# A new order of one head pair's work on all engines of an attention and mixture-of-experts kernel

## The chip, the core and the metric

The kernel runs on one core of a Trainium2 chip. It uses five engines with instruction streams of their own: TensorE (PE in the profile; its weight loads are listed apart, as PEld), VectorE (DVE), ScalarE (ACT), GpSimd (POOL) and SyncE (SP), which issues most of the DMAs. Each engine works through its instructions in the order in which the program wrote them, and waits where one needs a result of another engine. The metric is the time of one execution on the device in microseconds.

## The reference

Attention over 8 batches of 8 heads, 576 positions and 64 columns a head, with a learned bias (a small network of one hidden layer of 32, fed with log distances) that depends on the positions alone, and behind it a mixture of 8 experts, of which each token takes the best one, weighted with its probability `gate_w`.

```python
def _attn_ref(q, k, v, w1, b1, w2):
    scores = scale * np.matmul(q, k.transpose(0, 1, 3, 2))
    ...
    scores = scores + bias.transpose(2, 0, 1)[None, :, :, :]
    scores = scores - np.max(scores, axis=-1, keepdims=True)
    attn = np.exp(scores)
    attn = attn / (np.sum(attn, axis=-1, keepdims=True) + 1e-09)
    return np.matmul(attn, v).astype(np.float32)

def _moe_ref(x, modality_id, w_gate, modality_bias, w1, w2):
    logits = x @ w_gate + modality_bias[modality_id]
    e_idx = np.argmax(logits, axis=1)
    ...
    for e in range(E):
        h = np.maximum(x[mask] @ w1[e], 0.0)
        out[mask] = gate_w[mask, None] * (h @ w2[e])
```

## The kernel before

The kernel has three stages: a table of the bias is built (to about 65 us), attention runs over 32 pairs of heads (to about 602 us), and the experts' products follow. The change lies in the attention stage.

A pair of heads is two heads of one batch, side by side on the 128 partitions. Its 576 rows are cut into five chunks: chunks 0 to 3 of 128 rows, for each head on its own, and chunk 4, the last 64 rows of both heads together. One pair takes these steps, each with a letter in the order table. A capital starts a step on TensorE, and the small letter of the same step is the copy of its result out of PSUM.

- P0, P1, P2: q, k and the last rows of both are transposed (`prep`). H (ScalarE) writes the high part of the result, and G (VectorE) the low part; scores are made of three products of these parts.
- S0 to S4: the scores of a chunk (`scores`, L411), followed on VectorE by one pass a head that adds the bias and finds the row's extreme (`biased`, L434). The scores of both heads stand in `sps0` and `sps1`; S4 uses `sps0` alone. The passes write to one of four slots of `Eb`.
- E: the exponential of one chunk and head on ScalarE, in place (`exps`, L448). C: a copy of the last 64 columns on GpSimd (`compact`, L453).
- T0 to T4: the transposes of a chunk (`etrans`, L322, for chunk 4 L462). R and N: those of the last 64 columns (`rtrans`, L322, and `rtrans4`, L499). Their copies are t, r and n (L327 on ScalarE, L329 on VectorE).
- A0 to A3: four column pieces of the product with v (`av`, L523), 128, 144, 160 and 144 columns wide (`CUT`). Copied by a.
- L and V: loads of q and k, and of v, issued by SP. X, Y, O, Z and D: steps of the routing of a finished batch, which run beside the following pairs: Y logits and ranks, X their transposes and the token rows', O small operations on VectorE, Z scatters issued by GpSimd, D stores of the token rows.

The order in which the program writes all this is a table, `ORDER`: five strings, walked through once for each pair n by `attention`. A + behind a step means the pair n+1, a - the pair n-1, two signs two pairs. What follows the colon is the PSUM place of a step, or for a small letter the engine of the copy (a ScalarE, v VectorE; without it the default, both engines with one bank each for t and r, and ScalarE for a and n). TensorE's results besides the scores have four PSUM banks: `eps0` and `eps1` (e, or e0, e1), and `xps0` and `xps1` (x). T0 to T3 fill both banks of a letter, and an A takes one bank. Whoever fills a bank waits until the copy of what stood there is done. Other work hangs on the ends of the five strings by the string's number: the late blocks of the bias table at the first pair, and the first tables, row loads and weights of the experts' stage at the last four.

Of the kernel before, what the change touches and what calls it, by code (L numbers as in the profile page):

```python
# [23 lines left out]
D = 64  # L24
H = 8
NP = H // 2
HID = 32
S4 = S // 4
# [81 lines left out]
class Attn:  # L110
# [155 lines left out]
    def attn_early(self, st, rst):  # L266
# [22 lines left out]
        for k in range(2):  # L289
# [3 lines left out]
            qk = cp.tile([P, 2, P], F32, name=f"qkrem{k}")  # L293
            nc.vector.memset(qk, 0.0)
            self.qkrem.append(qk)
        self.qraw, self.kraw, self.vmain, self.E, self.rem, self.sums, self.xT = {}, {}, {}, {}, {}, {}, {}

    def attn_late(self, st):

# [212 lines left out]
    def av(self, n, part, u):  # L512

        nc = self.nc
        if part == 0:
            self.xT[n] = self.xTb[n // NP % 2][:, n % NP, :]
        v, eT, rT = self.vmain[n], self.eTs[n % 2], self.rT
        sl = slice(self.CUT[part], self.CUT[part + 1])
        ps = self.banks[u[0]][int(u[1])][:, 0 : sl.stop - sl.start]
        for k in range(5):  # L520
            for h in range(2):
                o = slice(64 * h, 64 * h + 64)
                nc.tensor.matmul(  # L523
                    ps[o, :],
                    v[:, h, k, :] if k < 4 else self.vrem[n % 2][:, o],
                    eT[:, h, k, sl] if k < 4 else rT[:, sl],
                    start=k == 0,
                    stop=k == 4,
                    tile_position=(0, 64 * h),
                    skip_group_check=True,  # L530
                )
        if part == 3:
            del self.vmain[n]
        dst = self.xT[n][:, sl]
        return lambda by=0: self.copy(by, dst, ps)

    def first_steps(self, route):
# [34 lines left out]


    ORDER = (
# [5 lines left out]
    )  # L580

    def attention(self):
# [47 lines left out]
        for n in range(n_pair + 2):  # L630
            for u in range(5):
# [5 lines left out]
                for op in self.ORDER[u].split():  # L637
# [9 lines left out]
                    elif op in ("x", "y"):  # L647
                        self.route_evac(op.upper())
                    elif 0 <= m < n_pair and not (n > n_pair and op[0] in "CV"):
                        pair[op[0]](m, *(int(x) for x in op[1:].strip("+-")), *([to] if to else []))  # L650
        while self.scatters:
            self.route_scatter()

# [989 lines left out]
```

## Time and profile before

| | |
|---|---|
| median of 3 runs | 1063.31 us (1060.08 to 1065.63) |
| the profiled execution | 1065.25 us, of which the span from the first to the last instruction is 1063.5 us |
| granted TensorE clock, mean | 0.988 of full speed |
| TensorE, matmuls | 1003.6 us busy, 94% of the span |
| TensorE, weight loads | 843.5 us, 79% |
| VectorE | 749.6 us, 70% |
| ScalarE | 683.5 us, 64% |
| GpSimd | 216.1 us, 20% |

Busy time is the union of the spans of an engine's instructions. Matmuls are pipelined, so that the next one starts before the last has ended, and the end of a matmul is modelled: the distance between two starts tells more than a length. In the rows, `xps<-idf,kraw 64*128 64x64` is a matmul into `xps` whose weights are 64 rows by 128 columns of the array; in brackets stands how long the engine had been idle, and what ended that.

### The profile page before, as it was taken

To read this page: it belongs to the slowest core of one execution; us is meant where nothing else is said; L and a number is where in the kernel's file an instruction comes from. 1 tells how busy PE (TensorE), PEld (TensorE's weight loads), DVE (VectorE), ACT (ScalarE), POOL (GpSimd) and SP (SyncE) were. 2 spreads that over 40 slices of the span, in tenths; PEclk is the share of its full clock that TensorE was granted. 3 is DMA by queue.
4 is the path that set the end of the run, shared out by engine and by line. 5 is a ranking of instruction groups with operands and counts; after the bars stand their busy time and mean duration, and the time that the engine had idled before them with its cause. 6 is when DMAs were issued, how large, how long until landed. Compare 5 with 4: busy or idle time off the path is not lost. (4 is left out here: it accounts for less than half of the span.)

```text
span 1063.5 us, 29967 instructions
## 1 busy us (share of the span) xinstructions
PE 1003.6 (94%) x11606; PEld 843.5 (79%) x11606; DVE 749.6 (70%) x1785; ACT 683.5 (64%) x1576; POOL 216.1 (20%) x371
## 2 busy tenths in 40 slices
PE   6978999998999999999998899999999999999996
PEld 3447888887888788887877788888888798988995
DVE  7976778877788787888887466985545455555554
ACT  6776787876878777887877454455535355454453
POOL 0000111212222122231323322421111112111120
PEclk9998999999999999999999999999999999999999
DMA  6973222324424334232337101224455511111111
GB/s 164 216 161 67 65 59 57 93 60 75 91 69 78 61 77 86 69 87 62 93 78 180 47 31 41 66 68 136 137 194 199 180 42 60 40 50 41 43 59 32
DMA packets 125036, 93.49 MB, mean 88 GB/s; under 512 B 94097, under 2 KB 102673, under 8 KB 124884
## 3 DMA queue, kind: packets, MB, share of 16 engines
q1 hardware_dynamic: 117268, 71.19, 26.6%
q0 software_dynamic: 7520, 20.30, 6.2%
q8 instruction: 93, 1.52, 0.8%
q14 instruction: 59, 0.48, 0.2%
q10 hardware_dynamic: 96, 0.00, 0.0%
HBM read 141.40 MB, written 19.38 MB: 151 GB/s over the span
## 5 line engine op out<-in xcount | busy, mean ns | idle before, releaser
L448 ACT ACTIVATE Eb<-Eb,mn 128x576 f32<-128x576 f32 x288 | 224.6, 787 | 17.5 <-DVE mn L434 17.1
L434 DVE CUSTOM_DVE_ANT_0 Eb<-sps,NBm 128x576 f32<-128x576 f32 x256 | 183.6, 754 | 20.8 <-PE sps L411 14.3
L411 PE MATMUL sps<-QK 64*128 64x288 f32 x1536 | 151.6, 316 | 16.0 <-ACT QK L334 7.4
L1259 PE MATMUL p<-QK,w1hi 128*128 128x256 f32 x1152 | 162.8, 284 | 1.3 <-ACT w1hi L1232 1.3
L523 PE MATMUL eps<-eT,vraw 128*64 128x144 f32 (+2 forms) x2048 | 156.6, 296 | 5.2 <-ACT eT L327 4.2
L1259 PEld LDWEIGHTS p<-QK,w1hi 128*128 128x128 f32 x1152 | 149.1, 192 | 7.8 <-issue 5.0
L523 PEld LDWEIGHTS eps<-eT,vraw 128*64 128x64 f32 x2048 | 121.7, 139 | 30.6 <-ACT eT L327 14.2
L411 PEld LDWEIGHTS sps<-QK 64*128 64x128 f32 x1536 | 115.8, 190 | 29.1 <-ACT QK L334 10.9
L1262 DVE SCALAR_TENSOR_TENSOR hl<-p,hh 128x512 fp32r<-128x512 f32 x72 | 49.6, 689 | 119.8 <-ACT hh L1261 118.0
L1261 ACT ACTIVATE hh<-p 128x512 fp32r<-128x512 f32 x72 | 43.0, 597 | 123.7 <-PE p L1259 108.3
L329 DVE COPY eT<-eps 128x512 f32<-128x512 f32 x128 | 88.0, 688 | 44.4 <-PE eps L322 40.5
L453 POOL COPY rem<-Eb 128x128 f32<-128x128 f32 x128 | 37.3, 292 | 337.4 <-ACT Eb L448 291.8
L322 PE MATMUL eps<-idf,Eb 64*128 64x64 f32 x2048 | 93.8, 227 | 7.2 <-ACT xTb L327 2.2
L1226 DVE TENSOR_TENSOR w2lo<-NBm,w2hi 128x1024 fp32r<-128x1024 f32 x72 | 89.3, 1240 | 15.2 <-ACT w2hi L1225 14.9
L1285 POOL DMA_INDIRECT out<-mo,idt x36 | 36.6, 1016 | 281.5 <-ACT mo L1284 258.9
L1259 PE MATMUL p<-QK,w1lo 128*128 128x256 f32 x576 | 92.7, 283 | 1.0 <-DVE w1lo L1233 1.0
L322 PEld LDWEIGHTS eps<-idf,Eb 64*128 64x128 f32 x2048 | 80.6, 141 | 11.9 <-ACT xTb L327 5.1
L1226 DVE TENSOR_TENSOR w1lo<-NBm,w1hi 128x1024 fp32r<-128x1024 f32 x72 | 84.9, 1221 | 3.5 <-ACT w1hi L1225 1.0
L1276 PE MATMUL xps<-w2hi,hh 128*128 128x512 f32 x208 | 83.0, 399 | 0.0
L1276 PE MATMUL xps<-w2hi,hl 128*128 128x512 f32 x208 | 81.4, 392 | 0.8 <-DVE hl L1262 0.8
L1259 PEld LDWEIGHTS p<-QK,w1lo 128*128 128x128 f32 x576 | 79.4, 192 | 1.4 <-DVE w1lo L1233 1.4
L327 ACT COPY eT<-eps 128x512 f32<-128x512 f32 x128 | 77.1, 602 | 3.3 <-PE eps L322 2.4
(254 smaller groups left out, 1756.8 us busy)
## 6 DMA issues: line engine op xcount, KB each, us to landing
NBm<-moe_w SPq DMA_DIRECT2D x20, 2048.0 KB
NBm<-moe_w SPq DMA_DIRECT2D x40, 1024.0 KB
NBm<-moe_w SPq DMA_DIRECT2D x32, 512.0 KB
NBm<-xTb SPq DMA_DIRECT2D x32, 288.0 KB
qraw<-q SPq DMA_DIRECT2D x64, 128.0 KB
kraw<-k SPq DMA_DIRECT2D x64, 128.0 KB
vraw<-v SPq DMA_DIRECT2D x32, 256.0 KB
xg<-xrb SPq DMA_DIRECT2D x28, 258.0 KB
```

The costliest lines, as they stand in the source:

```text
L322: self.nc.tensor.transpose(ps[r][0:n, col : col + 64], x[o, :], self.idf[o, o])
L327: self.nc.scalar.copy(out, ps)
L329: self.nc.vector.tensor_copy(out, ps)
L411: nc.tensor.matmul(self.sps[h or 0][:, half, 0:HS], QD[:, a, :] if h is None else QK[o, 0, a, P * c : P * c + P], QK[o, 1, b, ks], start=i ...
L434: nc.vector.tensor_tensor_reduce(out=e.rearrange("p (t w) -> p t w", t=2), in0=ps, in1=nb.rearrange("p (t w) -> p t w", t=2), scale=1.0, s ...
L448: self.nc.scalar.activation(e, e, AF.Exp, bias=mn, scale=-1.0, accum_out=sm)
L523: nc.tensor.matmul(ps[o, :], v[:, h, k, :] if k < 4 else self.vrem[n % 2][:, o], eT[:, h, k, sl] if k < 4 else rT[:, sl], start=k == 0, st ...
L1226: self.nc.vector.tensor_tensor(l, w, h.bitcast(F32), op=ALU.subtract)
L1259: nc.tensor.matmul(ps[:, a, :], w[:, c, fs], x[:, c, :], start=i == 0, stop=i == len(ops) - 1)
L1261: nc.scalar.activation(hh[:, sl, :], ps, AF.Relu)
L1262: nc.vector.scalar_tensor_tensor(hl[:, sl, :], ps, 0.0, hh[:, sl, :].bitcast(F32), op0=ALU.max, op1=ALU.subtract)
L1276: nc.tensor.matmul(ps, h[:, f, sl], m[:, f, :], start=i == 0, stop=i == len(ops) - 1)
```

## The change

`ORDER` is written anew. The steps of a pair are the same, and so is what each computes. In the new table
- A2 and A3 of pair n-2 follow each other, in e0 and x0; before, T3 and S1 stood between them, and A3 used e0;
- P2, P0 of the next pair stand behind S2 as before, but their parts H and G follow before S3, and P1 stands right behind S3; before, it stood behind S4;
- T2 and T1 of pair n stand behind S4, in e and x; T0 (in x) and T3 of the pair before (in e) stand behind S1, with T4;
- the exponentials of chunks 3 and 4 go to the next pair's first string, between the copies t2 and t1;
- A1's and A3's copies are ScalarE's now, and half of R's is VectorE's;
- the routing's X and Y have one place each in other strings, and the loads of q and k stand in the fourth string.

`av` no longer takes part 0 as the first and part 3 as the last: it sets its destination at each part, and counts the parts. Behind the loop the stores that are still waiting are issued.

```diff
     def av(self, n, part, u):
...
-        if part == 0:
-            self.xT[n] = self.xTb[n // NP % 2][:, n % NP, :]
+        self.xT[n] = self.xTb[n // NP % 2][:, n % NP, :]
+        self.av_done[n] = self.av_done.get(n, 0) + 1
...
-        if part == 3:
+        if self.av_done[n] == 4:
             del self.vmain[n]
...
     ORDER = (
-        "T2-:e t2- L++ S0 A2--:e0 a2--:a Y:e1 y X:x E0 T3-:e",
-        "x t3- S1 A3--:e0 N-:e1 E0 E1 n- E1 a3--:v T4-:x R-:x T0:e C0 C1 Z r-:a O",
-        "t4-:a t0 S2 O A0-:e1 a0-:a E2 P2+:x E2 P0+:x",
-        "H2+ T1:e H0+ V t1 S3 E3 C2 G0+ A1-:e1",
-        "a1-:v E3 S4 P1+:x H1+ G1+ G2+ O Z C3 O E4 D",
+        "E3- t2- E3- S0 O t1- E4- A2--:e0 A3--:x0 a2--:a E0 E0 C3- X:e O x R-:x r- S1 a3-- T4-:e t4-:a",
+        "T0:x E1 T3-:e t0 t3- E1",
+        "S2 P2+:x P0+:x",
+        "N-:e1 H0+ G0+ A0-:e1 E2 O E2 n-:a L++ S3 P1+:x Z a0- A1-:e0 V H1+ D H2+ G1+ C0 Y:e1",
+        "y G2+ S4 a1- C2 O Z T2:e T1:x C1",
     )
...
+        self.route_store()
         while self.scatters:
             self.route_scatter()
```

What stands in a row on TensorE, from A2 of a pair to the transposes behind S1 (here at pair 15; `Eb` holds the scores, `eT` their transposes, `rem` the last columns, `rT` the transposed ones). Before:

```order
L523 MATMUL eps0_739<-eT1_106,vraw13_4762 64x160 x8
L523 MATMUL eps0_739<-rT_107,vrem1_114 64x160 x2
...
L322 MATMUL eps0_739<-idf_62,Eb_88 128x64
...
L411 MATMUL sps0_737<-QK1_73 128x288
...
L523 MATMUL eps0_739<-eT1_106,vraw13_4762 64x144 x8
L523 MATMUL eps0_739<-rT_107,vrem1_114 64x144 x2
L499 MATMUL eps1_740<-idf_62,Eb_88 64x64 x2
L462 MATMUL xps0_77<-idf_62,Eb_88 128x64 x4
...
L322 MATMUL xps0_77<-idf_62,rem14_0_4993 128x64
```

A2 is followed by T3 into the same bank, then S1, A3, N, T4 and R; T0 comes next, and S2. The same stretch after:

```order
L523 MATMUL eps0_739<-eT1_106,vraw13_4776 64x160 x8
L523 MATMUL eps0_739<-rT_107,vrem1_114 64x160 x2
L523 MATMUL xps0_77<-eT1_106,vraw13_4776 64x144 x8
L523 MATMUL xps0_77<-rT_107,vrem1_114 64x144 x2
...
L322 MATMUL xps0_77<-idf_62,rem14_0_5092 128x64
...
L411 MATMUL sps0_737<-QK1_73 128x288
...
L462 MATMUL eps0_739<-idf_62,Eb_88 128x64 x4
...
L322 MATMUL xps0_77<-idf_62,Eb_88 128x64
...
L322 MATMUL eps0_739<-idf_62,Eb_88 128x64
```

A3 has moved up behind A2, into the other bank, R ahead of S1, and T4, T0 and T3 stand between S1 and S2, T4 and T3 in the same bank.

On ScalarE, around the parts of the next pair's q and k (`QK0` from `xps`, L336 with the scale for q, L334 for k; `mn15_6` is pair 15's chunk 3, first head, `mn15_8` chunk 4). Before:

```order
L336 ACTIVATE QK0_72<-xps0_77 128x4x64
L336 ACTIVATE QK0_72<-xps1_78 128x4x64
L327 COPY eT1_106<-eps0_739 128x8x64
L448 ACTIVATE Eb_88,sums15_5187<-Eb_88,mn15_6_5406 128x576
L448 ACTIVATE Eb_88,sums15_5187<-Eb_88,mn15_7_5408 128x576
L334 CAST QK0_72<-xps0_77 128x4x64
L334 CAST QK0_72<-xps1_78 128x4x64
L448 ACTIVATE Eb_88,sums15_5187<-Eb_88,mn15_8_5433 128x576
L327 COPY eT1_106<-eps0_739 128x8x64
L327 COPY xTb1_98<-eps0_739 128x160
```

The parts of k come behind both exponentials of chunk 3, and are followed by that of chunk 4, by T2's copy and by A2's. After:

```order
L336 ACTIVATE QK0_72<-xps1_78 128x4x64
L448 ACTIVATE Eb_88,sums15_5162<-Eb_88,mn15_4_5317 128x576
L448 ACTIVATE Eb_88,sums15_5162<-Eb_88,mn15_5_5319 128x576
L327 COPY rT_107<-eps1_740 128x64
L327 COPY xTb1_98<-eps1_740 128x128
L334 CAST QK0_72<-xps0_77 128x4x64
L334 CAST QK0_72<-xps1_78 128x4x64
L336 ACTIVATE QD0_108<-xps0_77 128x64
...
L327 COPY xTb1_98<-eps0_739 128x144
L448 ACTIVATE Eb_88,sums15_5162<-Eb_88,mn15_6_5378 128x576
```

The parts of k stand behind the exponentials of chunk 2 and the copies of N and A0, ahead of A1's copy, and the exponential of chunk 3 comes behind all of them.

## Rows read from the trace of the kernel before

**Rows 1.** The page: busy time of each engine, share of span, instructions.

```profile
PE 1003.6 (94%) x11606; PEld 843.5 (79%) x11606; DVE 749.6 (70%) x1785; ACT 683.5 (64%) x1576; POOL 216.1 (20%) x371
```

**Rows 2.** Windows: busy time in plain pairs; last TensorE clock, DMA share, GB/s.

```profile
129.00:145.00 16.00, 15.02 (x241) 12.83 (x243) 12.24 (x36) 13.07 (x40) 1.18 (x4) 1.00 0.24 57
```

**Rows 3.** Timeline, TensorE, one pair: start, length, engine, line, tiles, count, idle before.

```profile
111.73 1.06 PE L411 MATMUL sps<-QK,QD 128*128 128x288 f32 x6
112.73 0.46 PE L322 MATMUL xps<-idf,kraw 64*128 64x64 f32 x8
113.03 0.66 PE L322 MATMUL eps<-idf,Eb 64*128 64x64 f32 x16
113.92 1.44 PE L411 MATMUL sps<-QK 64*128 64x288 f32 x12 [0.24 <-ACT QK L334]
115.29 1.31 PE L523 MATMUL eps<-eT,vraw 128*64 128x160 f32 x16
...
117.27 0.71 PE L322 MATMUL eps<-idf,Eb 64*128 64x64 f32 x16 [0.39 <-ACT xTb L327]
117.78 1.04 PE L411 MATMUL sps<-QK 64*128 64x288 f32 x12
118.76 1.20 PE L523 MATMUL eps<-eT,vraw 128*64 128x144 f32 x16
...
120.03 0.28 PE L499 MATMUL eps<-idf,Eb 128*64 128x64 f32 x4
120.25 0.47 PE L462 MATMUL xps<-idf,Eb 64*128 64x64 f32 x8
120.55 0.42 PE L322 MATMUL xps<-idf,rem 64*128 64x64 f32 x8
120.80 0.69 PE L322 MATMUL eps<-idf,Eb 64*128 64x64 f32 x16
121.27 1.07 PE L411 MATMUL sps<-QK 64*128 64x288 f32 x12
...
125.54 1.20 PE L523 MATMUL eps<-eT,vraw 128*64 128x144 f32 x16
...
126.92 1.06 PE L411 MATMUL sps<-QK,QD 128*128 128x288 f32 x6
```

**Rows 4.** Timeline, TensorE: routing steps of two later pairs.

```profile
552.93 1.18 PE L780 MATMUL eps<-xTb,wgb 128*32 128x512 f32 x16
...
554.70 0.46 PE L322 MATMUL xps<-idf,xrb 64*128 64x64 f32 x8 [0.39 <-ACT xrb L327]
...
571.23 1.31 PE L523 MATMUL eps<-eT,vraw 128*64 128x160 f32 x16
...
572.74 0.71 PE L322 MATMUL xps<-idf,xTb 64*128 64x64 f32 x16
573.29 0.66 PE L322 MATMUL eps<-idf,Eb 64*128 64x64 f32 x16
```

**Rows 5.** Timeline, VectorE: the two passes after S1 of rows 3.

```profile
118.96 0.76 DVE L434 CUSTOM_DVE_ANT_0 Eb<-sps,NBm 128x576 f32<-128x576 f32 x1 [0.22 <-PE sps L411]
...
119.64 0.75 DVE L434 CUSTOM_DVE_ANT_0 Eb<-sps,NBm 128x576 f32<-128x576 f32 x1
```

**Rows 6.** Groups by line, ScalarE: busy, mean ns of one, idle before.

```profile
L448 ACT ACTIVATE Eb<-Eb,mn 128x576 f32<-128x576 f32 x288 | 224.6, 787 | 17.5 <-DVE mn L434 17.1
...
L327 ACT COPY rT<-xps 128x256 f32<-128x256 f32 x64 | 20.2, 368 | 0.4 <-PE xps L322 0.4
...
L327 ACT COPY xTb<-eps 128x128 f32<-128x128 f32 x64 | 17.8, 279 | 86.2 <-PE eps L523 81.8 <-PE xps L322 3.4 <-DVE xTb L329 0.9
```

**Rows 7.** Timeline, TensorE: S4 of the sixth and of the tenth pair.

```profile
157.29 0.79 PE L411 MATMUL sps<-QK,QD 128*128 128x288 f32 x4
...
220.62 0.79 PE L411 MATMUL sps<-QK,QD 128*128 128x288 f32 x4
```

**Rows 8.** Timeline, TensorE: the first A after the last S4.

```profile
587.40 2.35 PE L523 MATMUL eps<-eT,vraw 128*64 128x160 f32 x16 [1.72 <-ACT eT L327]
```

More of the change, by code (lines that the diff above doesn't have):

```diff
@@ L295, in attn_early @@
             self.qkrem.append(qk)
-        self.qraw, self.kraw, self.vmain, self.E, self.rem, self.sums, self.xT = {}, {}, {}, {}, {}, {}, {}
+        self.qraw, self.kraw, self.vmain, self.E, self.rem, self.sums, self.xT, self.av_done = {}, {}, {}, {}, {}, {}, {}, {}
     def attn_late(self, st):
```

## The prediction, made before the changed kernel was run

> **What bounds the kernel now.** I read the busy times first, then a 16 us window of the attention stage, then TensorE's timeline through one pair of heads, piece by piece, and last the rows of VectorE that a score block waits for. The page says TensorE 94% busy, VectorE 70%, ScalarE 64% [rows 1]; the window in the plain middle says 15.02 us of TensorE in 16, 13.07 of ScalarE, 12.24 of VectorE, at full granted clock [rows 2]. So TensorE sets the pace, and the others are not far below. But its busy time is the union of modelled spans, and a matmul that stands waiting for its operand counts as busy, so 94% doesn't mean that 6% is all there is to gain. The timeline of a pair shows it better, by the distance from one piece's start to the next one's [rows 3]. One pair without routing takes 126.92 - 111.73 = 15.19 us. I call the pieces by their letters in the table (S scores, T transposes of a chunk, A a quarter of the product with v, R and N the remainder's transposes, P transposes of q, k or their rests). The first line of rows 3 is S4.
>
> Three places in that pair are waits:
> - T2 starts at 113.03, S0 at 113.92: 0.89 us, where the same sixteen transposes ahead of S2 take 121.27 - 120.80 = 0.47. Wait 0.42: S0 needs the high part of the new k, which ScalarE has only just copied, since k was transposed one piece earlier.
> - S0 to A2 takes 1.37, S1 to A3 0.98: S0 stops in its middle 0.39 more, for the low part of k from VectorE.
> - A2 to T3 takes 117.27 - 115.29 = 1.98. The same 160-column piece, followed by the transposes of a routing step in the other bank, takes 572.74 - 571.23 = 1.51 [rows 4]. Wait 0.47: T3 goes into the bank that A2 has just filled and needs its eviction.
>
> Together 1.28 us. The work alone is 15.19 - 1.28 = 13.91 us a pair.
>
> **The change, part by part.** Nothing is added to or taken from TensorE's work. VectorE hands over two copies a pair (A1's and A3's) and takes one half of R's.
>
> (a) q and k in mid-pair: P2 and P0 stand after S2 now, and P1 after S3; the high and low parts are done by ScalarE and VectorE right behind. Between P1 and the S0 that needs it lie A1, S4, T2 and T1: 1.27 + 1.0 + 0.47 + 0.47 = 3.2 us by the starts in rows 3, where there was one T. The two waits at S0 go: -0.81. Both parts of k together took 0.47 + 0.42 + 0.39 = 1.3 us from T2's start on. Now VectorE first has S3's two passes, which end 2.6 us after S3's start (below), about when A1 ends (0.87 + 0.30 + 1.27); from there to S0 are S4, T2 and T1, 1.9 us, so the parts are done in time. Without that cover the 0.81 would be back. The loads of q and k stand later in the code, but they are issued by SP, whose only waits are for free buffers, and the two sets of buffers let it run most of a pair ahead; I cost this at nothing.
>
> (b) A3 behind A2, in banks e0 and x0, with the remainder's R next in x's other columns: nothing follows A2 into its own bank. T3 goes to two pieces before S2. The wait at T3 goes: -0.47.
>
> (c) Fewer turns between two kinds of matmul. A (and N) uses the array as 128x64 tiles, S and the transposes as 64x128, S4 as a whole. Before, four times a pair an A or N is followed by another kind; now three. What one costs: A1 to S4 is 126.92 - 125.54 = 1.38, A3 to N, same width and same kind after it, 1.27: 0.11 [rows 3]. The entries into A fall from four to three as well; no row has an S that is not followed by an A, so the entry has no price of its own here: between 0 and the 0.11 of the exit; I take 0.11, since it is the same turn the other way. Sum -0.22 (bounds -0.11 and -0.22; fewer turns can't cost anything). The Trainium skill, "TensorEngine Tiling (Array Packing)", Key Properties, says that a change of tiling mode drains TensorE, while another tile of one mode doesn't. By that rule both turns cost, and the pair gains 0.22; if only the exit cost, 0.11, and the forecast would be 3 us later. The exit row agrees; no row here shows the entry.
>
> (d) What is late next: S2. Between S1 and S2 now stand only T4, T0 and T3: S1 0.98 less the turn 0.11, T4 0.30, T0 0.47, T3 0.51 [rows 3], 2.15 us. S2 writes the same two score banks as S1, and they come free when VectorE has added the bias to both: S1 starts at 117.78, its first pass at 118.96, its second at 119.64 and 0.75 long [rows 5], so 120.39, 2.61 after S1. New wait 0.46 a pair. T3 has a second condition: it goes into T4's bank, and both of T4's copies are on ScalarE now. T4 ends 0.87 + 0.47 = 1.34 after S1's start (its own span is 0.47), two copies of this width at 0.37 us [rows 6] end by 2.1; T3 starts into the second bank then and ends by 2.6. It ties with VectorE, no second cost.
>
> (e) Other distances between score blocks: S0 to S1 has A2, A3 and R between, S2 to S3 has P2 and P0 (at least P1's 0.30), N (0.22) and A0 (16 columns less than A1: 1.2), with S2's 0.87 some 2.6. S3 to S4 has P1 and A1, 2.4, and S4 to S0 has T2 and T1, 1.0 + 0.94; but S4 fills one bank only and has one pass. These are near ties: I add 0.05 for them (bounds 0 and 0.2).
>
> (f) ScalarE: busy 13.07 of 16 is 12.4 us a pair [rows 2]; two copies of 0.28 more, one of 0.37 less [rows 6]: 12.6. That fits into the 14.2 found below, at 89%.
>
> So a plain pair goes from 15.19 to 15.19 - 0.81 - 0.47 - 0.22 + 0.46 + 0.05 = 14.2 us, a gain of 1.0; there are 30 intervals between the second pair's S4 and the last one's: -30 us.
>
> (g) Routing. Four pairs with a batch's routing take 220.62 - 157.29 = 63.33 [rows 7], four plain ones 60.76: 2.6 extra. Its pieces by rows 4: the logits 554.70 - 552.93 = 1.77, of which 0.39 is a wait; turning them, like R's transposes and two more [rows 3], 0.3; two steps of rows 573.29 - 572.74 = 0.55 each, a half one, and the ranks, 0.5 together. That is 3.3 without the wait (1.38 + 0.3 + 2 x 0.55 + 0.5). 0.5 to 0.7 of it lay in the wait at T3, which I have already taken away; and the rank step's three small operations on VectorE now stand ahead of S4's pass, and S0 waits for that. So a batch costs about 3.6 now, 1.0 more; seven batches: +7. Bounds: +0 (the new wait at S2 hides some) and +10.
>
> (h) The end. After the last S4 there is one wait of 1.72 us, and the A behind it spans 2.35 us, where the same piece spans 1.31 in a plain pair [rows 3, 8]: 2.8 us in all. Now T2 and T1, two A's and R stand between there, so most goes: -2 (bounds 0 and -3). The late blocks of the bias at the start, and everything after the attention, I take as unchanged.
>
> **Sum.** The profiled execution took 1065.25 us (span 1063.5). -30 + 7 - 2 = -25: 1040. The median of the three runs, 1063.31, is 1.9 below that execution; the forecast for a median is 1038.
>
> **Rivals.**
> 1. TensorE is full already. If 94% busy [rows 1] were work, an order could give nothing: 1063. For it: VectorE and ScalarE wait for TensorE more than the other way round. Against it: the same pieces have two lengths within one pair [rows 3]. The Trainium skill, "Perfetto Trace Analysis", Identifying the Most-Contended Engine, says that TensorE's matmul busy share is no measure of how near it is to its roof and names the share of weight loads instead; here that is 79%, and the trace agrees. Chance 0.08.
> 2. ScalarE becomes the bound. It must do its work in single file, and at 89% a few waits in its queue (for T2 before it can go on with the exponentials, for A2 before those of the new pair) are passed on. Each 0.1 us a pair is 3 us. With 0.5 of it a pair takes 14.7: 1053. For it: 12.6 us of work and the waits in new places; against it: the waits last as long as a part of a TensorE piece. Chance 0.17.
> 3. The bank wait moves to T3 and grows. T4's two copies stand in ScalarE's queue behind two exponentials (0.79 each, [rows 6]), half of R and A3's copy, and T3, S2 and all behind them wait. If ScalarE reaches T4 late by w, each pair loses w. The gain of 25 is gone at w = 0.8; past 0.5% slower it is from w = 1.0, and with both exponentials late (1.6 us) the time is 1063 - 25 + 48 = 1086; a middle case, w = 1.1, gives 1071. For it: ScalarE's load, and that evictions of A2 held T3 up before. Against it: these two exponentials need S0's passes, which end 2.6 us after S0's start, and A2, A3, R and S1 then still stand between, some 2.5 us and more. The Trainium skill, "Perfetto Trace Analysis", Identifying Performance Opportunities (Optimization Strategy), says that a gap that repeats can mean that SBUF or PSUM is too small for the next tile. By that rule the gap at T3 comes back in another place, as here; the wait at T3 in rows 3 is such a gap, and the change adds no bank. Chance 0.10.
> 4. More than forecast: the wait at S2 is partly hidden and routing costs nothing extra. 30 x 0.3 + 7 = 16 less: 1022. Chance 0.10.
>
> **How the numbers follow.** Forecast 0.55 (1028 to 1048); the rivals 0.08, 0.17, 0.10, 0.10. A measurement of this kernel can tell about 0.5%, 5.3 us, from no change. Faster: 0.55 + 0.10 + most of rival 2 = 0.81. Same: rival 1 and the bad end of rival 2, 0.09. Slower: 0.10. The range reaches from rival 4's time to a little past rival 2's, and leaves out rivals 1 and 3: 1022 to 1057.
>
> **What would show it.** S0's twelve matmuls start within 0.5 us of T1's start and run through; A3 starts 1.4 us after A2; S1 to S2 is 2.6 us, and the wait there is put down to VectorE (my step (d)) or to ScalarE (rival 3). Plain pairs last 14.2 us; ScalarE is busy for 14 us and more in 16. The forecast is wrong if S1 to S2 is over 3.2 us, or if ScalarE has no idle time left in a plain pair.

## The result, and the profile after

The changed kernel takes 1036.09 us, the median of 4 runs (1032.96 to 1039.33); the kernel before, run beside it on the same chip, 1063.1 us (median of 4 runs, 1060.08 to 1065.63). The ratio is 0.9747, 95% interval 0.9708 to 0.9787: 27 us less, where 25 were forecast (1038, range 1022 to 1057).

The busy times on the page of the changed kernel, to be read beside [rows 1], and a window of its plain pairs, beside [rows 2] (busy time of TensorE, its weight loads, VectorE, ScalarE, GpSimd; then granted clock, DMA share, GB/s):

```profile
PE 985.9 (96%) x11606; PEld 851.0 (83%) x11606; DVE 736.0 (71%) x1753; ACT 691.5 (67%) x1608; POOL 213.3 (21%) x371
```

```profile
97.00:113.00 16.00, 16.00 (x275) 14.56 (x270) 12.12 (x33) 14.00 (x43) 3.46 (x8) 1.00 0.33 79
```

TensorE's instructions are the same 11606, ScalarE has 32 more and VectorE 32 fewer. TensorE now counts as busy for 16.00 of 16 us, at full granted clock, and still there is a wait in every pair, as the next view shows: a matmul that stands for its operand is busy by this count. The weight loads' share rose from 79% to 83%, for the most part because the span is shorter.

One plain pair, that is one ahead of the first routing, TensorE's timeline, the answer to [rows 3] (start, length, tiles, count):

```profile
106.95 1.05 PE L411 MATMUL sps<-QK,QD 128*128 128x288 f32 x6
...
108.48 0.66 PE L322 MATMUL xps<-idf,Eb 64*128 64x64 f32 x16
108.96 1.05 PE L411 MATMUL sps<-QK 64*128 64x288 f32 x12
109.94 1.31 PE L523 MATMUL eps<-eT,vraw 128*64 128x160 f32 x16
...
111.35 1.15 PE L523 MATMUL xps<-eT,vraw 128*64 128x144 f32 x16
...
112.68 0.46 PE L322 MATMUL xps<-idf,rem 64*128 64x64 f32 x8
112.95 1.04 PE L411 MATMUL sps<-QK 64*128 64x288 f32 x12
113.83 0.41 PE L462 MATMUL eps<-idf,Eb 64*128 64x64 f32 x7
...
114.13 0.66 PE L322 MATMUL xps<-idf,Eb 64*128 64x64 f32 x15
114.69 0.93 PE L322 MATMUL eps<-idf,Eb 64*128 64x64 f32 x15
115.43 0.38 PE L411 MATMUL sps<-QK 64*128 64x288 f32 x1
...
115.63 1.06 PE L411 MATMUL sps<-QK 64*128 64x288 f32 x11
116.40 0.35 PE L322 MATMUL xps<-idf,qkrem 64*128 64x64 f32 x2
...
116.68 0.46 PE L322 MATMUL xps<-idf,qraw 64*128 64x64 f32 x8
...
121.04 1.05 PE L411 MATMUL sps<-QK,QD 128*128 128x288 f32 x6
```

S4 to S4 is 121.04 - 106.95 = 14.09 us, against 15.19. S0 (108.96) starts 0.48 after T1 and runs through in 0.98; A3 comes 1.41 after A2. S1 to S2 is 2.48 us to S2's first matmul and 2.68 to its second, the one into the other head's bank; T3 takes 0.74 of it where a T without a wait takes 0.47.

The two engines that S2 and T3 wait for: VectorE's passes of S1, and ScalarE's copies of T4.

```profile
114.13 0.76 DVE L434 CUSTOM_DVE_ANT_0 Eb<-sps,NBm 128x576 f32<-128x576 f32 x1 [0.50 <-PE sps L411]
...
114.81 0.75 DVE L434 CUSTOM_DVE_ANT_0 Eb<-sps,NBm 128x576 f32<-128x576 f32 x1
```

```profile
114.26 0.65 ACT L327 COPY eT<-eps 128x256 f32<-128x256 f32 x2 [0.44 <-PE eps L462]
```

The second pass ends at 115.56, and S2's second matmul starts at 115.63. T4's copies end at 114.91. T3 goes into the same two banks: its first transpose, into the bank that is copied first, starts at 114.69, and the next, into the other, at 114.97.

Where the time went, by starts of S4, TensorE's timeline of both kernels: that of the second pair, of the pair at which the first batch's routing begins (the sixth before, whose row is the first of [rows 7], the fifth after, since the logits stand one step earlier now), that of 24 pairs later, the last one, and the first product of the experts.

The kernel before:

```profile
96.55 1.06 PE L411 MATMUL sps<-QK,QD 128*128 128x288 f32 x6
...
547.85 1.06 PE L411 MATMUL sps<-QK,QD 128*128 128x288 f32 x6
...
583.98 1.06 PE L411 MATMUL sps<-QK,QD 128*128 128x288 f32 x6
...
603.38 1.21 PE L1259 MATMUL p<-QK,w1hi 128*128 128x256 f32 x8 [1.29 <-ACT w1hi L1232]
```

The changed kernel:

```profile
92.86 1.06 PE L411 MATMUL sps<-QK,QD 128*128 128x288 f32 x6
...
135.15 1.06 PE L411 MATMUL sps<-QK,QD 128*128 128x288 f32 x6
...
499.44 1.05 PE L411 MATMUL sps<-QK,QD 128*128 128x288 f32 x6
...
550.83 1.04 PE L411 MATMUL sps<-QK,QD 128*128 128x288 f32 x6
...
571.84 1.47 PE L1260 MATMUL p<-QK,w1hi 128*128 128x256 f32 x6 [1.30 <-ACT w1hi L1233]
```

| part | before, us | after, us | difference | forecast |
|---|---|---|---|---|
| up to the second S4 | 96.55 | 92.86 | -3.7 | 0 |
| 30 intervals: 30 plain pairs of 15.18 and 14.10 | 455.5 | 422.9 | -32.6 | -30 |
| what 24 pairs with six batches' routing take above plain ones (all waits there included) | 26.2 | 26.0 | -0.2 | +6 |
| what the last pairs take above plain ones (2 before, 3 after) | 5.8 | 9.1 | +3.3 | +1 |
| last S4 to the experts' first product | 19.40 | 21.01 | +1.6 | -2 |
| experts and what follows | 460.1 | 459.4 | -0.7 | 0 |
| span | 1063.5 | 1031.2 | -32.3 | -25 |

The 24 pairs took 547.85 - 157.29 = 390.56 us before, 24 x 15.18 = 364.4 of it plain, and 499.44 - 135.15 = 364.29 after, 24 x 14.10 = 338.3 plain; what follows up to the last S4, 36.13 for two pairs and 51.39 for three. The two profiled executions lie 32.3 apart and the medians 27.0: the one of before, 1065.25, was 2 us above its median, the one of after, 1032.96, 3 us below. So the column of differences holds some 5 us more than the medians show.

### The profile page after: what moved, and what is told of

The parts are those of the page before. It is cut to its first block, busy times and chain, and to the rows that moved or that the text cites. A ratio compares the mean times of both kernels' runs of the same rounds, so it can differ in the third digit from the quotient of the medians.

```text
span 1031.2 us, 30009 instructions
## 1 busy us (share of the span) xinstructions
PE 985.9 (96%) x11606; PEld 851.0 (83%) x11606; DVE 736.0 (71%) x1753; ACT 691.5 (67%) x1608; POOL 213.3 (21%) x371
## 5 line engine op out<-in xcount | busy, mean ns | idle before, releaser
L411 PE MATMUL sps<-QK 64*128 64x288 f32 x1536 | 143.1, 310 | 2.7 <-DVE mn L434 2.0
L411 PEld LDWEIGHTS sps<-QK 64*128 64x128 f32 x1536 | 112.9, 186 | 11.1 <-DVE mn L434 4.5
L523 PE MATMUL eps<-eT,vraw 128*64 128x128 f32 (+2 forms) x1536 | 113.7, 290 | 1.4 <-ACT xTb L327 0.9
L523 PEld LDWEIGHTS eps<-eT,vraw 128*64 128x64 f32 x1536 | 89.8, 137 | 8.9 <-issue 4.4
L327 ACT COPY eT<-eps 128x512 f32<-128x512 f32 (+1 forms) x128 | 58.4, 481 | 34.5 <-PE eps L322 16.4
L1226 ACT CAST w2hi<-NBm 128x1024 fp32r<-128x1024 f32 x72 | 74.9, 1040 | 0.0
L1226 ACT CAST w1hi<-NBm 128x1024 fp32r<-128x1024 f32 x72 | 72.4, 1062 | 0.0
L1285 ACT ACTIVATE mo<-xps,NBr 128x512 f32<-128x512 f32 x26 | 17.9, 690 | 72.1 <-issue 65.9
```

The source lines that it names most:

```text
L327: self.nc.scalar.copy(out, ps)
L411: nc.tensor.matmul(self.sps[h or 0][:, half, 0:HS], QD[:, a, :] if h is None else QK[o, 0, a, P * c : P * c + P], QK[o, 1, b, ks], start=i ...
L523: nc.tensor.matmul(ps[o, :], v[:, h, k, :] if k < 4 else self.vrem[n % 2][:, o], eT[:, h, k, sl] if k < 4 else rT[:, sl], start=k == 0, st ...
L1226: self.nc.scalar.copy(h, w)
```

## The experiments

All times are medians, beside runs of the kernel before on the same chip. Diffs are of the table ORDER unless another line is shown. "Plain pair" is S4 to S4 ahead of the first routing.

### One wait at a time, put into the kernel before

**other_bank: T3 in the other bank (step b alone).**

```diff
-"... a2--:a Y:e1 y X:x E0 T3-:e",
+"... a2--:a Y:e1 y E0 T3-:x X:e",
```

> The kernel before, with two letters changed: T3 goes into the other bank (x), the routing's transposes X into e and behind T3. Theory (step b of the prediction): T3's wait of 0.47 us is A2's eviction alone. A2 to T3 falls from 1.98 to 1.51 us, the plain pair from 15.19 to 14.72, 31 pairs give 14.6 us: 1048. Rival: the same time is waited for further on (at S1, which needs the score banks that VectorE empties 2.6 us after S0's start): S0 to S1 would then stay at 3.86 us and the time at 1063. From S0's start A2 and T3 leave 1.37 + 1.51 + 0.51 = 3.4 us, above 2.6, so the rival gives nothing by that sum.

Measured: 1063.09 us (10 runs) against 1062.99; ratio 0.9987, 0.9965 to 1.0009. No difference, and yet the plain pair fell from 15.18 to 14.72, as expected to 0.01 us. TensorE's timeline, A2 and T3 of a plain pair, then A2, T3, X and S1 of a pair with routing:

```profile
115.02 1.31 PE L523 MATMUL eps<-eT,vraw 128*64 128x160 f32 x16
...
116.53 0.72 PE L322 MATMUL xps<-idf,Eb 64*128 64x64 f32 x16
```

```profile
499.89 1.31 PE L523 MATMUL eps<-eT,vraw 128*64 128x160 f32 x16
...
501.40 0.71 PE L322 MATMUL xps<-idf,Eb 64*128 64x64 f32 x16
501.95 0.67 PE L322 MATMUL eps<-idf,xTb 64*128 64x64 f32 x16
502.43 1.30 PE L411 MATMUL sps<-QK 64*128 64x288 f32 x12
```

What follows: the wait of 0.47 us behind A2 is real, and the other bank removes it. But in a pair with routing the transposes X stood between A2 and T3 already [rows 4, from 572.74 on], and covered A2's eviction; a batch is four pairs, and there is an X in each. So the wait existed in the four intervals ahead of the first routing, which is where [rows 3] was read, and in few others: those four fell by 60.73 - 58.87 = 1.9 us, and the 24 pairs with routing behind them, 389.76 us against 390.56, by no more than two executions differ. Neither theory of mine had that.

**qk_mid: q and k in mid-pair (step a alone).**

```diff
-"T2-:e t2- L++ S0 A2--:e0 ...",
+"T2-:e T1-:x t2- t1- S0 E4- A2--:e0 ...",
-"t4-:a t0 S2 O A0-:e1 a0-:a E2 P2+:x E2 P0+:x",
-"H2+ T1:e H0+ V t1 S3 E3 C2 G0+ A1-:e1",
-"a1-:v E3 S4 P1+:x H1+ G1+ G2+ O Z C3 O E4 D",
+"t4-:a t0 S2 O P2+:x P0+:x H0+ G0+ A0-:e1 E2 a0-:a E2 L++",
+"V S3 P1+:x A1-:e0 H1+ H2+ G1+ C2",
+"G2+ S4 a1-:a E3 E3 O Z C3 O D",
```

(R's copy is split over the two engines too.)

> The kernel before, with step (a) alone and what it takes along: P2 and P0 ahead of A0, P1 ahead of A1, T1 behind T2, a1 on ScalarE, the exponentials of block 3 and 4 later; T3 stays behind A2 in A2's bank, A3 behind S1. Theory (step a): both waits for k at S0 go and nothing takes their place: S0 starts 2.0 us after S4 and runs through in 0.98, the plain pair is 15.19 - 0.81 = 14.38, 31 pairs give 25 us: 1038. The wait of 0.47 at T3 stays. Rival: the late k was the cover of another wait (VectorE's pass of S4 and the evictions of T2 and T1 now stand in a row ahead of S0's passes, ScalarE has the exponentials of block 3, T2, T1 and a1 in a row): A2 or T3 then waits longer, pair 14.7 or more, 1048 and more.

Measured: 1043.51 against 1062.99; ratio 0.9834, 0.9797 to 0.9871. TensorE, one plain pair: P2 and P0, then S4, S0 and A2:

```profile
115.94 0.51 PE L322 MATMUL xps<-idf,qkrem 64*128 64x64 f32 x2
...
116.49 0.47 PE L322 MATMUL xps<-idf,qraw 64*128 64x64 f32 x8
...
120.74 1.06 PE L411 MATMUL sps<-QK,QD 128*128 128x288 f32 x6
...
122.76 1.05 PE L411 MATMUL sps<-QK 64*128 64x288 f32 x12
123.74 1.31 PE L523 MATMUL eps<-eT,vraw 128*64 128x160 f32 x16
```

S0 starts 2.02 us after S4 and runs through in 0.98, as in the changed kernel: both waits for k are gone, and the wait at T3 stays (A2 to T3 1.97). The plain pair is 14.56 to 14.74, not 14.38, since a smaller wait came in: P2 takes 0.55 us, 0.28 at the same place in the changed kernel (116.40 to 116.68). The 30 intervals fell by 15.2 us, 0.51 a pair; with P2's 0.3 that is step (a)'s 0.8. So (a) is the large part of this change, and it holds in pairs with routing too (24 of them take 379.77 us, 10.8 less), which (b) does not. Not all of the 19.5 us are step (a)'s, though: the edit also moves the loads L and A1's copy, and 5.0 us of the gain lie ahead of the second S4 (91.51 against 96.55), where the loads matter, as loads_late and loads_mid show below.

**both: the two together, A3 left between S1 and S2.** The diffs of other_bank and qk_mid in one kernel.

> The kernel before with both: q and k in mid-pair as in qk_mid, and T3 in the other bank as in other_bank. A3 stays between S1 and S2, so that S1 to S2 is 0.98 + 1.28 + 0.21 + 0.30 + 0.25 + 0.47 = 3.5 us of work and VectorE's 2.6 us are covered there, which they are not in the changed kernel. Theory (waits only, steps a, b and d): 15.19 - 0.81 - 0.47 = 13.9 us a plain pair, 0.2 less than the changed kernel's 14.09, with one more turn of TensorE between two kinds of matmul: 1030. Rival (the changed kernel's fewer turns and other lags are what counts): 14.2 or more, 1040 and more.

Measured: 1036.61 against 1062.99; ratio 0.9757, 0.9739 to 0.9774, not to be told from the changed kernel's. The plain pair is 14.10, between the theory (13.9) and the rival (14.2 or more): it has no wait at S2 and four stretches of products with v a pair instead of three, and loses 0.2 at P2 (0.47). A table with other places for A3, R, N and T3 thus gives the same time. In the pairs with routing the profiled execution loses to the changed kernel's (30 intervals 465.0 us, 458.0 there), at both ends of the attention it gains (the second S4 at 91.21; the experts' first product 19.0 us behind the last S4).

**both_t4_split: half of T4's copy on VectorE.**

```diff
-"t4-:a t0 S2 ...",
+"t4- t0 S2 ...",
```

> The kernel both, with one more edit: the second half of T4's copy on VectorE instead of ScalarE. In both, P2 behind S2 takes 0.47 us (0.35 to its second transpose) where it takes 0.12 in the kernel before: it goes into T4's bank and waits for T4's second copy, which ScalarE ends 0.2 us after P2's start. Theory: the wait of 0.25 to 0.35 goes, a plain pair falls from 14.10 to 13.85, 30 pairs give 7.5 us: 1029, below the changed kernel. Rival: VectorE, with 0.4 us more ahead of S2's passes, makes S3 wait as much: 14.1, 1036.

Measured: 1038.89 against 1063.19; ratio 0.9761, 0.9734 to 0.9788. The same as both. P2 takes 0.41 instead of 0.47, the plain pair 14.05 instead of 14.10. The wait was smaller than I had put it, 0.2 and not 0.35, since the 0.12 of the kernel before is a P2 behind A0; and T4's second copy was no more than a third of it. What the rest is was not found. My theory of it fell, and the rival did not come true either (S3 is not later).

### Undoing parts of the changed kernel

**late_k: P1 back behind S4, T1 behind S0.**

```diff
-"E3- t2- E3- S0 O t1- ...",
+"E3- t2- E3- S0 T1-:x O t1- ...",
-"... L++ S3 P1+:x Z a0- A1-:e0 V H1+ D H2+ G1+ C0 Y:e1",
-"y G2+ S4 a1- C2 O Z T2:e T1:x C1",
+"... L++ S3 Z a0- A1-:e0 V D H2+ C0 Y:e1",
+"y G2+ S4 P1+:x H1+ G1+ a1- C2 O Z T2:e C1",
```

> The changed kernel with step (a) undone: P1 back behind S4 with its high and low parts, T1 from ahead of S0 to behind it. Theory (step a): S0 waits for k again as in the kernel before, start 2.19 us behind S4, 1.37 long; with T1's 0.47 behind it and P1's 0.33 gone from between S3 and S4, a plain pair goes from 14.09 to 14.09 - (2.01 + 0.98) + (2.19 + 1.37 + 0.47 - 0.33) = 14.8, 30 pairs give 21 us: 1057. Rival (the other moves give the gain, k's lateness is hidden elsewhere): 14.3 or less, 1042 or less.

Measured: 1176.08 against 1063.19, and this says nothing on the theory. T1 behind S0 reads the exponentials of block 1 from a buffer that S0's own pass fills again (four buffers for five blocks), so this kernel computes other attention values and sends other tokens to the experts. And the edit put A1's copy behind the high part of k in ScalarE's queue, so that T2, which goes into A1's bank, came 1.38 us after P1, another wait than the one to be restored. What remains is a limit of the order: T1 can stand behind S4, as in the changed kernel, but not behind S0, and that needs P1 out of bank x by then.

**copies_back: the copies on their engines of before (step f).**

```diff
-"... R-:x r- S1 a3-- T4-:e t4-:a",
+"... R-:x r-:a a3--:v S1 T4-:e t4-:a",
-"y G2+ S4 a1- C2 ...",
+"y G2+ a1-:v S4 C2 ...",
```

> The changed kernel with the copies back on the engines of before: A1's and A3's on VectorE, both halves of R's on ScalarE. Theory (step f: ScalarE at 89% has time to spare, and the move of A1's copy is needed for another reason): taking 0.2 us a pair off ScalarE gains nothing; A1's copy on VectorE stands behind S3's two passes and the low parts, so that T2, which goes into A1's bank, starts about 0.3 us later: a plain pair 14.4, 1045. Rival (ScalarE is the bound): the pair falls below 14.09, 1033 or less. Third: nothing moves, 14.09, 1036.

Measured: 1055.78 against 1063.19; ratio 0.9913, 0.9880 to 0.9947. The plain pair is 14.38, and the 0.29 us are where they were expected, at T2. TensorE's T2, 1.35 us after S4 instead of 0.99, and what it waits for, VectorE's copy of A1 behind the low parts:

```profile
110.86 0.72 PE L322 MATMUL eps<-idf,Eb 64*128 64x64 f32 x16 [0.29 <-DVE xTb L329]
```

```profile
110.41 0.30 DVE L329 COPY xTb<-eps 128x144 f32<-128x144 f32 x1
```

ScalarE with less work gained nothing, so it isn't the bound. Copies of 0.3 us, whose move I had costed as nothing but ScalarE's time, are worth 0.29 x 30 = 9 us by the plain pair and 18 us (by the ratios) to 20 us (by the medians) in all. In the profiled execution, which lies 23 us above the changed kernel's, 10 more are in the pairs with routing, 2 ahead of the second S4 and 2 at the end; I did not follow them further, and waits there differ from one execution to the next.

**turn_between and turn_behind: the price of a turn (step c).** One transpose of 64x64 more a pair, between A2 and A3 or behind A3:

```diff
-"... A2--:e0 A3--:x0 ...",
+"... A2--:e0 U--:x A3--:x0 ...",
```

```diff
-"... C3- X:e O x R-:x ...",
+"... C3- U--:x X:e O x R-:x ...",
```

> The changed kernel with one more transpose of 64x64 in every pair, of the identity into columns that R overwrites, put between A2 and A3, so that TensorE leaves the products with v and goes back to them once more. Theory (step c: an exit and an entry cost about 0.1 us each): A2 to A3 grows by the transpose's own 0.03 and by 0.1 to 0.2, a plain pair from 14.09 to 14.25, 1041. Rival (turns cost nothing, what step c saw was something else): 14.12, 1037.

> The changed kernel with the same additional transpose of 64x64 behind A3, where R's transposes of the same kind follow: no further turn. Both theories: its own 0.03 us a pair, 14.12, 1037. The difference to turn_between is the price of one exit and one entry.

Measured: 1048.95 and 1040.18, against 1059.52 on that chip (ratios 0.9906, 0.9862 to 0.9950, and 0.9847, 0.9807 to 0.9887). The plain pairs are 14.42 and 14.14: one exit and one entry cost 0.28 us. TensorE's timeline, turn_between (A2, the transpose, A3), then turn_behind (A3, the transpose, R):

```profile
113.64 1.31 PE L523 MATMUL eps<-eT,vraw 128*64 128x160 f32 x16
...
115.15 0.24 PE L627 MATMUL xps<-idf 64*64 64x64 f32 x1
115.32 1.20 PE L523 MATMUL xps<-eT,vraw 128*64 128x144 f32 x16
```

```profile
113.13 1.15 PE L523 MATMUL xps<-eT,vraw 128*64 128x144 f32 x16
...
114.46 0.24 PE L627 MATMUL xps<-idf 64*64 64x64 f32 x1
114.47 0.48 PE L322 MATMUL xps<-idf,rem 64*128 64x64 f32 x8
```

A2 is followed after 1.51 us, in the changed kernel, where A3 is next, after 1.41: 0.10 for the exit. The transpose is followed by A3 after 0.17 us, by R after 0.01: 0.16 for the entry from a transpose. The transpose by itself costs hardly more than its place in the queue (14.14 against 14.09 a pair), and from its 64x64 tiles to R's 64x128 there is no price to be seen (0.01). The entry from a score block, which [rows 3] could not show and which is the one that the change removes, can be read in the changed kernel's plain pair above: S0, with A2 behind it, takes 109.94 - 108.96 = 0.98, S1, with T4 behind it, 113.83 - 112.95 = 0.88, so 0.10.

**n_and_last_y: work put into the new wait (step d), and the last logits out of the attention's end.**

```diff
-"... S1 a3-- T4-:e t4-:a",
+"... S1 a3-- T4-:e N-:e1 t4-:a n-:a",
-"N-:e1 H0+ G0+ A0-:e1 E2 O E2 n-:a L++ S3 ...",
+"H0+ G0+ A0-:e1 E2 O E2 L++ S3 ...",
@@ attention
-                        self.route_next(op, to)
+                        if not (op == "Y" and n > n_pair):
+                            self.route_next(op, to)
```

> The changed kernel with two edits. First, N (0.17 us, two turns of its own) goes from between P0 and A0 to behind T4, into the wait ahead of S2. Theory (step d: S2 comes 2.6 us after S1, bound by VectorE's two passes): S1 to S2 stays at 2.5 to 2.7 us, S2 to S3 falls by 0.17, a plain pair from 14.09 to 13.9, 30 pairs give 5 us. Rival (S2's wait is TensorE's own work or T3's bank): S1 to S2 grows by 0.2 to 0.35, the pair is the same or longer, up to 14.2. Second, the last batch's logits stay out of the attention's end, as in the kernel before: the last S4 to the first matrix product of the experts falls from 21.0 to 19.4 us, of which the stage behind gives 0.7 back. Together 1030 by the theory, 1036 and more by the rival.

Measured: 1040.33 against 1059.52; ratio 0.9834, 0.9806 to 0.9862. That is no better than the changed kernel, and not to be told from turn_behind (0.9847), the changed kernel but for one transpose, measured beside it on the same chip. The plain pair is 14.04, 0.05 less. N with its two turns adds 0.37 us to the work ahead of S2, and P2, the piece behind S2, comes 3.54 us after S1 instead of 3.45: 0.28 of the 0.37 went into the wait. What it saves between S2 and S3 is 0.15. So the wait is there and can be filled, as (d) has it, but I had counted on more. The longest wait lies elsewhere, in the second pair from the end. GpSimd, VectorE and TensorE there:

```profile
542.89 0.93 POOL L917 DMA_INDIRECT tab<-ids,pos  x1 [7.39 <-DMA tab<-ids,pos]
543.82 0.53 POOL L453 COPY rem<-Eb 128x128 f32<-128x128 f32 x2
```

```profile
544.15 0.76 DVE L434 CUSTOM_DVE_ANT_0 Eb<-sps,NBm 128x576 f32<-128x576 f32 x1 [5.35 <-POOL rem L453]
```

```profile
546.76 0.58 PE L322 MATMUL xps<-idf,rem 64*128 64x64 f32 x6 [4.58 <-DVE eT L329]
```

A scatter Z waits 7.39 us for the transfer of the scatter before it. The small copy C1 stands behind it in GpSimd's queue and holds the buffer into which VectorE's pass of the next S0 writes. The change put C1 there: the table of before has "C0 C1 Z" and only C3 behind a Z, whose buffer isn't filled again before the next S2; the new one has "C2 O Z T2:e T1:x C1". The changed kernel has the same wait at the same place:

```profile
542.66 0.40 PE L322 MATMUL xps<-idf,rem 64*128 64x64 f32 x6 [2.21 <-DVE eT L329]
```

So these two edits did not bring it. Its length differs from run to run: in turn_behind it is 5.22 us, and the last interval between two S4 takes 21.17 us there, 17.12 in the changed kernel and 21.66 in n_and_last_y.

**c_ahead_of_z: the copies C ahead of the scatters, T1's copy ahead of S0's passes.**

```diff
-"E3- t2- E3- S0 O t1- E4- ...",
+"E3- t2- E3- t1- S0 O E4- ...",
-"... S3 P1+:x Z a0- A1-:e0 V H1+ D H2+ G1+ C0 Y:e1",
-"y G2+ S4 a1- C2 O Z T2:e T1:x C1",
+"... S3 P1+:x C0 Z a0- A1-:e0 V H1+ D H2+ G1+ Y:e1",
+"y G2+ S4 a1- C2 C1 O Z T2:e T1:x",
```

> n_and_last_y with the order of two queues mended. On GpSimd the small copies C1 and C0 go ahead of the scatter Z in their step; on VectorE T1's copy goes ahead of S0's passes. Theory: in the second pair from the end of n_and_last_y a scatter waits 7.39 us for the transfer before it, C1 behind it frees the buffer that S0's pass writes, VectorE waits 5.35 and TensorE 4.58 us (2.21 in the changed kernel); in the first pair R waits 1.70 us in the changed kernel for T1's copy behind S0's passes. Both waits go, plain pairs stay at 14.04: the last interval between two S4 falls from 21.66 to about 17, the first from 15.45 to 14, together 6 us below n_and_last_y. Rival for the first: another wait on the scatter takes its place (the last interval stays above 20). Rival for the second: S0's passes, 0.2 us later in every pair, make S1 late and the plain pair grows to 14.2. As a ratio to the kernel before: 0.9834 for n_and_last_y, 0.978 by the theory; the changed kernel has 0.9747.

Measured: 1038.83 (6 runs) against 1066.72 on that chip; ratio 0.9742, 0.9717 to 0.9768. Both waits went: the last interval is 15.38 us instead of 21.66, the first 13.81 instead of 15.45, plain pairs stay at 14.04. The scatter itself still waits 7.59 us, but nothing hangs on it. Against n_and_last_y's 0.9834 that is a gain of about 0.9%, on two different chips; the two intervals account for 7.9 us, 0.7%. Against the changed kernel's 0.9747 nothing can be told: no version here is shown to be faster than the changed kernel.

### The loads of q and k, alone, in the kernel before

**loads_late and loads_mid.** L moved behind A1, or behind P0:

```diff
-"T2-:e t2- L++ S0 ...",
+"T2-:e t2- S0 ...",
-"H2+ T1:e H0+ V t1 S3 E3 C2 G0+ A1-:e1",
+"H2+ T1:e H0+ V t1 S3 E3 C2 G0+ A1-:e1 L++",
```

```diff
-"... E2 P2+:x E2 P0+:x",
+"... E2 P2+:x E2 P0+:x L++",
```

> The kernel before, with only the loads of the next q and k (L) moved from behind T2's eviction to behind A1, as in the changed kernel. The first pair's S4 to the second pair's takes 19.27 us in the kernel before and 15.84 in the changed one; a plain pair differs by 1.09 only, so 2.3 us are from something else. Theory: S4's pass of the first pair waits 2.07 us for the last rows of the bias table, whose transfer stands behind these loads in SyncE's queue. Then this edit alone brings 2 to 2.3 us at the first pair and nothing in a plain pair: 1061. Rival: the 2.3 us come from the lower clock of that stretch (granted 0.68 of full speed between 81 and 97 us, 0.88 in the changed kernel), which follows from another wait, and the edit changes nothing there: 1063.

> The kernel before, with only the loads of the next q and k (L) moved from behind T2's eviction to behind P0, ahead of the loads of v and of the routing's stores (loads_late put them between the two). Theory: the first pair's S4 to the second's falls from 19.27 to 14.6 us as in loads_late, and without the routing's stores behind the loads no pair waits for a store: 1058.5. Rival: loads anywhere later than before collide with the stores: 1063 and more.

Measured: loads_late 1079.21 against 1062.99 (ratio 1.0178, 1.0136 to 1.0221); loads_mid 1059.13 against 1063.19 (0.9952, 0.9930 to 0.9973). VectorE's pass of the first pair's S4 in the kernel before, then ScalarE's copy of a row block for the experts in loads_late:

```profile
80.65 0.76 DVE L434 CUSTOM_DVE_ANT_0 Eb<-sps,NBr 128x576 f32<-128x576 f32 x1 [2.07 <-POOL xrb L703]
```

```profile
211.23 0.37 ACT L327 COPY xrb<-xps 64x256 f32<-64x256 f32 x1 [4.79 <-DMA xg<-xrb]
```

The wait of 2.07 us at the first pair's S4 comes from where the loads stand, since moving them and nothing else removes it (the profile puts it down to a GpSimd step; the bias rows that the pass reads were issued behind such loads of q and k). With them the first interval falls from 19.27 to 14.62 us (loads_late) or 16.69 (loads_mid, at a granted clock of 0.79 from 81 to 97 us; 1.00 in loads_late, 0.68 before, 0.89 in the changed kernel). The changed kernel's 3.7 us at the start are for the most part two things: the first interval, 15.84, is 1.1 shorter as any plain pair is, and 2.3 more, which fits the place of the loads. That part of its 27 us I had costed at nothing. And the place matters: in loads_late the routing's stores are issued right behind the loads of v, q and k, a copy that needs a store's buffer goes on some 9.5 us later (issue 201.72, copy 211.23), and such copies wait for 4.79 us here, up to 5.8 elsewhere.

## Why the prediction came out, step by step

The time was right (1038 forecast, 1036.09 measured), and so were the plain pair (14.2, measured 14.09) and its main mechanism, the waits at S0 and T3 that go and the one at S2 that comes. That the sum came out within 2 us is in part luck: it hides errors of both signs.

- **(a)** Right, -0.81 a pair. S0 starts 0.48 after T1 and runs through in 0.98; qk_mid shows it alone. What the step said of its cover holds too: the high and low parts of k are done some 1.0 us before S0 (VectorE's last at 107.94).
- **(b)** Right in the row, wrong in the count. -0.47 is what a pair without routing gains (other_bank), but I applied it to 30 pairs from a row read ahead of the first routing, and in pairs with an X it was hidden already. For 24 pairs that is 11 us of forecast gain that this step did not bring. Rows 4, which I used as the price without a wait, show just that. My step (g) allowed 0.5 to 0.7 us a batch for it; with four X a batch it is up to 4 x 0.47 = 1.9.
- **(c)** Right that both turns cost: 0.22 was forecast for an exit and an entry, and they are worth 0.20 if the entry is one from a score block (0.10 and 0.10 by the rows), 0.28 as turn_between had it, with an entry from a transpose. The Trainium skill, "TensorEngine Tiling (Array Packing)", Key Properties, says that a change of mode drains TensorE, and both turns do cost here, as by that rule. The change from 64x64 tiles to R's 64x128, which is one too, showed no price (0.01), and there the measurement decides.
- **(d)** Right: the wait at S2 is 0.45 by the pieces (T0 0.09, T3 0.27, S2 0.09 longer than without a wait), 0.46 was forecast, and S2's two parts, one behind T3, which T4's copies hold, the other behind VectorE's second pass, start 0.2 us apart (115.43 and 115.63), the tie that I described. n_and_last_y could fill 0.28 of it. Rival 3, T3 held by ScalarE, is this wait at a quarter of a us; it never grew. The Trainium skill, "Perfetto Trace Analysis", Identifying Performance Opportunities (Optimization Strategy), says that a repeating gap can mean too little SBUF or PSUM. By that rule the gap at T3's bank comes back in another place, and so it did, at T3 and S2, with 0.45 for 0.47; the 0.81 at S0, which was no wait for a bank, did not.
- **(e)** 0.05 of near ties: none is seen.
- **(f)** Right: ScalarE is busy 14.00 of 16 us, 88%, and has idle time in every plain pair; taking copies off it (copies_back) lost time. Rival 2 is out. But why the copies moved I had not seen: A1's copy on VectorE holds T2 up by 0.29.
- So a plain pair goes by 15.19 - 0.81 - 0.47 - 0.28 + 0.45 = 14.08. That this meets 14.09 is luck to about 0.2 us, for with 0.20 for the turns it is 14.16, and pieces left out changed by as much both ways: P2 takes 0.28 behind S2 where it took 0.12 behind A0, P0 0.39 for 0.31; S3, which has P1 behind it instead of A1, takes 0.90 for 1.04 or more.
- **(g)** Wrong: +7 forecast. Routing with all that disturbs these pairs costs 26 us over six batches in both kernels. My 2.6 us a batch for before came from its first batch, one of the less disturbed; the six average 26.2 / 6 = 4.4. In a batch with few other waits routing takes 2.6 us above plain pairs before (157.29 to 220.62) and 2.9 after (440.14 to 499.44): +0.3 a batch where I had +1.0. Nor do the 11 us of (b) show in the total: the 24 pairs fell by 26.3 us, 1.09 each, as much as plain ones. By (a), (c) and (d) alone such a batch falls by 4 x (0.81 + 0.28 - 0.45) = 2.6 us; it fell by 63.33 - 59.30 = 4.0. Of the 1.4 more, 0.9 are two waits that went: the logits' 0.39 [rows 4], which I had left out of the new price, and one of 0.5 in one pair of a batch, at A3, which I had not seen. TensorE's S1 and A3 there, in the kernel before:

```profile
180.18 1.33 PE L411 MATMUL sps<-QK 64*128 64x288 f32 x12
181.69 1.20 PE L523 MATMUL eps<-eT,vraw 128*64 128x144 f32 x16 [0.18 <-ACT eT L327]
```

  S1 to A3 is 1.51 instead of 0.98: A3 needs T3's copies, and these stood behind the copies of X's result. The rest was not taken apart. The last pairs lost 3.3 us instead, of which 2.2 is the scatter's wait. That is a queue that I had listed (Z and C on GpSimd) without asking what the scatter waits for.
- **(h)** Wrong in sign: -2 forecast, +1.6 measured. The 1.72 us wait of [rows 8] went, as said (0.17 now). Others took its place. TensorE's timeline of the changed kernel behind the last S4, two of them (the 1.30 ahead of 571.84 is above):

```profile
565.36 1.31 PE L523 MATMUL eps<-eT,vraw 128*64 128x160 f32 x16 [0.86 <-ACT xTb L327]
...
569.10 1.23 PE L781 MATMUL eps<-xTb,wgb 128*32 128x512 f32 x16 [0.60 <-DVE xrb L329]
```

  The last batch's logits (569.10) now stand ahead of the experts too. With them out again the stretch took 20.1 us in n_and_last_y, but 22.4 in c_ahead_of_z, so how much of the 1.6 they are stays open.
- **The start**, taken as unchanged, gave 3.7 us: 1.1 is a plain pair's gain in the first interval, and 2.3 more in it fit the place of the loads, whose move alone took 4.7 (loads_late) and 2.6 us (loads_mid) off it.

TensorE was not full (rival 1), although the page now says 96%.

## What to carry to other kernels

Count a wait over the stretches in which it exists: a row from a plain stretch, times the number of all pairs, overstates it wherever other work stands in the gap, and an edit that removes it there gains nothing. An order of instructions is several orders at once; the small copies, loads and scatters that a table moves along need the same question as the large steps (what is this queue's next instruction waiting for, and whose buffer does it hold), and here they were worth 18 to 20 us (the copies' engines), 2 to 5 us (the loads, at the first pair) and 2 to 5 us (a copy behind a scatter). A total that is right to 2 us says little of its terms: here five of the table's six parts were 2 to 6 us off.

## What the runs showed of the hardware

- A turn of TensorE from 128x64 tiles to a transpose costs 0.10 us (1.51 against 1.41 behind A2), the turn back 0.16 from a transpose (0.17 against 0.01) and 0.10 from a score block (0.98 against 0.88).
- Both kernels have waits of 0.7 to 2.7 us in the routing part that I could not put down to the order, and they differ from version to version. The kernel before and other_bank have one in the same pair. ScalarE's high part of k there, in the kernel before:

```profile
241.66 0.65 ACT L334 CAST QK<-xps 128x256 fp32r<-128x256 f32 x2 [2.51 <-remote]
```

  ScalarE waits 2.51 us here and 2.75 in other_bank, and TensorE's S0 then 2.67 and 2.91, for P1, whose transposes TensorE's rows show 2.5 us earlier. It is open what these waits are. They may be a part of why two executions of one kernel, and two versions with the same plain pair, differ by several us.
